# Query transposes moved to other places of a row pair, weights turned earlier, two tap groups read together, and a tail's second rows asked earlier, in an E-Branchformer kernel

## The chip, the cores and the metric

One NeuronCore of a Trainium2 chip. The time is the device time of one launch in microseconds (us); medians and ranges are over several launches. The profile is one launch taken by the hardware profiler. Times in it count from the start of its span.

The engines: PE is TensorE's matmuls and PEld its weight loads, DVE is VectorE, ACT is ScalarE, POOL is GpSimd, and SP is the engine whose queue asks for most transfers. "L2057" is a line of the kernel. The changed kernel's lines stand one or two further down. Names such as X, pD, Sm or dhr are the program's own tiles: in the attention stage the PE writes scores to pS and pD, ACT and DVE make Pm and Sm of them, the PE adds products of these up in X ("X fills"), and acc takes X up. In a tail, gs and ug are rows that are read, dhr is the gradient dh read back, and EF and gr are sums for the weights' gradients.

## The reference

Forward and backward pass of one E-Branchformer layer (two batches, 4000 tokens, 144 channels, bf16), with the gradients of the input and of all seven weights:

```python
def _fwd_reference(x, w_qkv, w_att_out, w_mlp_in, dw_csgu, w_mlp_out, dw_merge, w_merge):
    xa = _layernorm(x)
    q, k, v = split(xa @ w_qkv)                       # cut
    attn = softmax(q @ k.T * D ** -0.5) @ v
    glob = attn @ w_att_out
    u, g = split(gelu(_layernorm(x) @ w_mlp_in))
    g = _layernorm(g); gc = sum of 5 shifted g * dw_csgu      # cut
    loc = (u * gc) @ w_mlp_out
    m = concat(glob, loc); m = m + (5 shifted m * dw_merge)   # cut
    return x + m @ w_merge
# reference(): the output and jax.vjp's gradients for x and the weights
```

## The kernel before

Each batch goes through three stages: a head, the attention stage (two thirds of the time), and a tail. The parts that the change touches, cut:

**Places.** In the attention stage, row blocks of 128 are worked in pairs of 16 places. At each place the PE does its fixed work, and a small scheduler may add one step of a task: of the local branch or of the query transposes.

```python
class Steps:
    def place(self, tensor=True):
        ...
            due = [t for t in self.tasks if t[1] is not None and (t[1][0] == 'P' or t[1][0] == 'L' and self.now % 2) and self._ready(t)]
            if due:
                self._step(min(due, key=lambda t: t[0]))
        self.now += 1
...
        def jit(g):                       # query transposes, 7 a batch
            ...
            for step in range(3):
                yield 'P', 2
                ...
                pj = ps_f.tile([128, 4, 128], BF, tag="f", name="pj")
                for j in range(4):
                    nc.tensor.transpose(pj[:, j, :], src[:, j, :], id_[:])
                nc.scalar.copy(jt[g][step][:], pj[:])
...
        # (row block of 0..7 half places) -> X fills (number, rows); three PSUM banks in all
        fills = {(0, 1): ((0, (0,)), (1, (0,))), (1, 0): ((0, (1,)), (1, (1,))), (1, 1): ((2, (0, 1)),), (2, 1): ((3, (0, 1)),), ...}
```

Three PSUM banks serve the X fills, the transposes and the local steps, least recently used first. Fills 0 and 1 of a pair are opened at place 1 and closed at place 2. Even fills are added up by DVE (`acc<-X,acc`), odd ones by ACT and POOL.

**The tail** runs in program order:

```python
            loads(0)                 # gs and ug rows of group 0
            load_dh(0)               # dhr: dh back from DRAM
            load_dh(1)
            loads(1)
            ...
            for h in range(NPR + 5):
                g, hf = divmod(h, 2)
                if 0 < h < NPR:
                    turn_dx2(*turn_dx(h))        # transposes of dhr and others
                if hf == 0 and 0 <= g - 2 < NGR - 1:
                    fill(g - 2)                  # reads r<-y and r<-u on ACT's queue
                if h == NPR + 1:
                    fill(NGR - 1)
                ...
                if h == NPR - 1:
                    spill_ef()                   # ACT copies EF out of four banks; gr takes two of them
```

**The head** of the first batch turns the weights and builds products of them:

```python
        # heads()
        WlT = self.turn(self.Wl, D, 0, D, "w_lT", pst)
        # phase_head: order of the first steps
                wts.heads(ps_t, ps_2, lambda: nrm.stats(0))
                nrm.power(0)
                wts.taps1(0)          # POOL: w_A<-w_lT,w_wr
                wts.keys(ps_t, ps_2)  # turns w_q and w_k, then the fused M
                nrm.shift(0)
                narrow(0)             # POOL: g<-gs, the narrow rows
                nrm.apply(0)
                wts.taps()            # DVE: w_A<-w_voT,w_wr, w_Bz
```

## Time and profile before

| | before |
|---|---|
| time, median of 3 (range) | 1273.08 us (1272.24 to 1273.53) |
| profiled span | 1269.4 us |
| PE busy | 1206.0 us, 95% |
| granted PE clock | 0.997; 1.00 in every stage, lower only after 1262 us |
| attention stages | 68 to 545 and 683 to 1155 us |
| PE waits for X behind DVE's acc | 4.4 us a stage |

How to read it: 95% of PE time is in use, so only its gaps are to be had. Lines such as `PE X L2057 <- DVE acc L2073` name the waiting instruction and what it waited for. The lines themselves are shown in the prediction below.

### The profile page before, as it was taken

To read this page: it belongs to the slowest core of one execution; us is meant where nothing else is said; L and a number is where in the kernel's file an instruction comes from. 1 tells how busy PE (TensorE), PEld (TensorE's weight loads), DVE (VectorE), ACT (ScalarE), POOL (GpSimd) and SP (SyncE) were. 2 spreads that over 40 slices of the span, in tenths; PEclk is the share of its full clock that TensorE was granted. 3 is DMA by queue.
4 is the path that set the end of the run, shared out by engine and by line. 5 is a ranking of instruction groups with operands and counts; after the bars stand their busy time and mean duration, and the time that the engine had idled before them with its cause. 6 is when DMAs were issued, how large, how long until landed. Compare 5 with 4: busy or idle time off the path is not lost.

```text
span 1269.4 us, 39810 instructions
## 1 busy us (share of the span) xinstructions
PE 1206.0 (95%) x15118; PEld 946.8 (75%) x15118; DVE 962.5 (76%) x3261; ACT 843.4 (66%) x2494; POOL 558.3 (44%) x1007
## 2 busy tenths in 40 slices
PE   7999999999999999989999999999999999998996
PEld 4667777777777777789886777777777777778984
DVE  7567788888788887857646678888888878875774
ACT  5777767776777666546567777777776776654542
POOL 7323444544445533357512254544544445325650
PEclk9999999999999999999999999999999999999998
DMA  7479898889998999978857998999898999998861
GB/s 212 100 142 179 147 157 159 161 150 159 162 160 149 164 164 157 158 205 218 222 160 139 156 162 143 155 161 170 152 166 155 157 163 154 158 162 197 243 172 25
DMA packets 633616, 205.43 MB, mean 162 GB/s; under 512 B 576719, under 2 KB 630948, under 8 KB 633380
## 3 DMA queue, kind: packets, MB, share of 16 engines
q1 hardware_dynamic: 626912, 197.46, 82.6%
q10 hardware_dynamic: 6500, 5.32, 1.8%
q8 instruction: 120, 1.97, 0.6%
q14 instruction: 84, 0.69, 0.2%
HBM read 46.11 MB, written 21.79 MB: 53 GB/s over the span
## 4 chain that ended last, share of the span: by engine, by line
PE 71%; DVE 13%; DMA 4%; ACT 4%; issue 4%; POOL 1%; SPq 0%; ACTq 0%; DVEq 0%; POOLq 0%
PE y L2035 15%; PE pS L1989 9%; PE X L2057 8%; PE X L2058 8%; PE pD L1989 7%; DVE Sm L1999 5%; PE pS L1985 5%; PE pb L1518 3%; PE pc L1693 2%; PE EF L2193 2%; PE po L2218 2%; DVE jg L1916 2%; DMA ug<-ug_d 1%; PE gr L2289 1%; DVE acc L2073 1%
## 5 line engine op out<-in xcount | busy, mean ns | idle before, releaser
L1999 DVE SCALAR_TENSOR_TENSOR Sm<-pD,Pm 128x500 bf16<-128x500 f32 x512 | 325.7, 673 | 81.3 <-PE pD L1989 46.0
L1997 ACT ACTIVATE Pm<-pS 128x500 bf16<-128x500 f32 x512 | 295.8, 586 | 39.4 <-PE pS L1989 36.3
L2057 PE MATMUL X<-Qs,Sm 128*128 128x144 bf16 x2048 | 285.8, 226 | 9.3 <-DVE acc L2073 8.9
L2070 POOL TENSOR_TENSOR acc<-xs,acc 128x432 f32<-128x432 f32 x150 | 168.5, 1124 | 281.7 <-ACT xs L2069 281.3
L2058 PE MATMUL X<-Bt,Pm 128*128 128x144 bf16 x2048 | 285.6, 226 | 0.8 <-DVE Bt L2022 0.8
L2058 PEld LDWEIGHTS <-Pm 128*128 128x128 bf16 x2048 | 200.2, 98 | 11.9 <-issue 11.4
L2057 PEld LDWEIGHTS <-Sm 128*128 128x128 bf16 x2048 | 200.1, 98 | 1.6 <-issue 1.0
L2035 PEld LDWEIGHTS <-PT 128*128 128x128 bf16 x2048 | 136.6, 98 | 31.0 <-issue 3.0
L2035 PEld LDWEIGHTS <-ST 128*128 128x128 bf16 x2048 | 136.4, 98 | 27.6
L2069 ACT COPY xs<-X 128x432 f32<-128x432 f32 x150 | 78.0, 520 | 111.6 <-PE X L2058 103.3
L2073 DVE TENSOR_TENSOR acc<-X,acc 128x432 f32<-128x432 f32 x180 | 104.0, 578 | 54.3 <-PE X L2058 53.7
L1997 ACT ACTIVATION_READ_ACCUMULATOR Pm<-pS 128x1 f32 x512 | 104.7, 205 | 0.0
L1985 PE MATMUL pD<-rb,QBr 16*128 16x500 bf16 x448 | 95.5, 378 | 4.0 <-DVE Sm L1999 3.5
L1989 PEld LDWEIGHTS <-BTm 128*128 128x128 bf16 x512 | 49.8, 98 | 59.9 <-issue 1.6
L1985 PE MATMUL pS<-rb,QBr 16*128 16x500 bf16 x448 | 91.9, 379 | 0.3
L1916 DVE SCALAR_TENSOR_TENSOR jg<-gnC,dgC 128x256 bf16<-128x256 bf16 x160 | 90.8, 568 | 1.2
L2045 POOL TENSOR_TENSOR B_t<-zd,yd 128x144 bf16<-128x144 f32 x64 | 34.1, 533 | 112.5 <-ACT zd L2044 112.2
L1989 PEld LDWEIGHTS <-QTm 128*128 128x128 bf16 x512 | 29.0, 97 | 72.2 <-issue 72.2
L1989 PE MATMUL pS<-ra,QTm 128*128 128x500 bf16 x256 | 76.5, 380 | 0.0
L1989 PE MATMUL pS<-rb,QTm 128*128 128x500 bf16 x256 | 76.5, 380 | 0.0
L2035 PE MATMUL y<-ra,PT 128*128 128x144 bf16 x1024 | 74.3, 226 | 1.4 <-ACT zd L2044 1.4
L2035 PE MATMUL y<-rb,PT 128*128 128x144 bf16 x1024 | 74.3, 226 | 1.4 <-ACT zd L2044 1.4
(638 smaller groups left out, 2878.6 us busy)
## 6 DMA issues: line engine op xcount, KB each, us to landing
gs<-in_grad_out_dram SPq DMA_DIRECT2D x24, 720.0 KB
dh_d<-dh SPq DMA_DIRECT2D x32, 144.0 KB
dhr<-dh_d SPq DMA_DIRECT2D x16, 288.0 KB
gs<-in_grad_out_dram SPq DMA_DIRECT2D x8, 540.0 KB
xg<-in_x_dram SPq DMA_DIRECT2D x21, 144.0 KB
dug_d<-dug SPq DMA_DIRECT2D x16, 144.0 KB
dug<-dug_d SPq DMA_DIRECT2D x32, 72.0 KB
ug_d<-ug SPq DMA_DIRECT2D x32, 72.0 KB
```

Source lines behind the costliest of these rows:

```text
L1518: nc.tensor.matmul(pb[:], goT[:, i * 128 + m:i * 128 + m + 128], W.GL[:, m, :, :].rearrange("p a b -> p (a b)"), start=(m == 0), stop=False)
L1916: nc.vector.scalar_tensor_tensor(jg[:], a_[:, m:m + 256], 1.0, d_[:, 2:258], op0=ALU.mult, op1=ALU.mult, accum_out=dws[:, p, m:m + 1])
L1985: nc.tensor.matmul(o_[h][:, 0:SC], jt[i // 4][2][rr, i % 4, :], S.XR[c2][rr, 0:SC], start=True, stop=False)
L1989: nc.tensor.matmul(o_[h][:, 0:SC], jt[i // 4][w][:, i % 4, :], S.xaT[:, c0:c0 + SC], start=False, stop=True)
L1997: nc.scalar.activation(P[:, pb, c1:c1 + SC], o_[h][:, 0:SC], ACT.Exp, accum_out=ld8[:, 0, n_:n_ + 1])
L1999: nc.vector.scalar_tensor_tensor(Sm[:, pb, c1:c1 + SC], o_[h][:, 0:SC], 1.0, P[:, pb, c1:c1 + SC], op0=ALU.mult, op1=ALU.mult, accum_out=l ...
L2035: nc.tensor.matmul(y[:, w, :], src[:, jj, :], S.xaa[:, j, :], start=(j == 0), stop=(j == NBK - 1))
L2057: nc.tensor.matmul(X[:, jj, :], Sm[:, i % NP, j * 128:(j + 1) * 128], Qs[:, i % 4, :], start=(kk == 0 and jj == 0), stop=False, skip_group ...
L2058: nc.tensor.matmul(X[:, jj, :], P[:, i % NP, j * 128:(j + 1) * 128], Bt[:, i % 4, :], start=False, stop=(kk == 1), skip_group_check=True)
L2069: nc.scalar.copy(xs[:, 0:nj, :], X[:, 0:nj, :])
L2070: nc.gpsimd.tensor_tensor(a_, xs[:, 0:nj, :], a_, op=ALU.add)
L2073: nc.vector.tensor_tensor(a_, X[:, 0:nj, :], a_, op=ALU.add)
```

## The change

Four parts, with their intents: (A) turn the query and key weights while another weight is still on its way; (B) keep the query transposes from the places where X fills hold two of three banks; (C) read the last two tap groups together, before the EF copies; (D) ask for the tail's second group of rows first.

```diff
@@ heads(), keys()                                               (A)
+        self.WqT = self.turn(W.Wqkv, D, 0, D, "w_qT", pst)
+        self.WkT = self.turn(W.Wqkv, D, D, D, "w_kT", pst)
         WlT = self.turn(self.Wl, D, 0, D, "w_lT", pst)
...
-        WqT = self.WqT = self.turn(W.Wqkv, D, 0, D, "w_qT", pst)
-        WkT = self.WkT = self.turn(W.Wqkv, D, D, D, "w_kT", pst)
+        WqT, WkT = self.WqT, self.WkT
@@ place(), jit()                                                (B)
-   ... t[1][0] == 'L' and self.now % 2) and self._ready(t)]
+   ... t[1][0] == 'L' and self.now % 16 > 2) and self._ready(t)]
...
-                yield 'P', 2
+                yield 'L', 1
@@ phase_tail()                                                 (D)
             loads(0)
+            loads(1)
             load_dh(0)
             load_dh(1)
-            loads(1)
...                                                              (C)
-                if hf == 0 and 0 <= g - 2 < NGR - 1:
+                if hf == 0 and 0 <= g - 2 < NGR - 2:
                     fill(g - 2)
-                if h == NPR + 1:
-                    fill(NGR - 1)
...
                 if h == NPR - 1:
+                    fill(NGR - 2)
+                    fill(NGR - 1)
                     spill_ef()
```

More of the change, by code (lines that the diff above doesn't have):

```diff
@@ L1766, in place @@
         if tensor:
-            due = [t for t in self.tasks if t[1] is not None and (t[1][0] == 'P' or t[1][0] == 'L' and self.now % 2) and self._ready(t)]
+            due = [t for t in self.tasks if t[1] is not None and (t[1][0] == 'P' or t[1][0] == 'L' and self.now % 16 > 2) and self._ready(t)]
             if due:
```

## The prediction

The "up to 0.4 us" for four issues is the author's estimate; in the profile before, the ACT queue's four reads between 619 and 624 us took 0.32 to 0.67 us each to ask.

> **What bounds the kernel now.** I read the page's busy shares first, then the chain of waits, then windows of the PE per stage, then the waits of the PE inside a long stage, and last the single instructions around the commonest of these waits. Busy shares and chain:
>
> ```profile
> PE 1206.0 (95%) x15118; PEld 946.8 (75%) x15118; DVE 962.5 (76%) x3261; ACT 843.4 (66%) x2494; POOL 558.3 (44%) x1007
> PE 71%; DVE 13%; DMA 4%; ACT 4%; issue 4%; POOL 1%; SPq 0%; ACTq 0%; DVEq 0%; POOLq 0%
> ```
>
> TensorE (PE) is busy 1206.0 of a span of 1269.4 us, and 71% of the chain is its own work. The change removes no matmul, so at most the 63.4 us of PE idle time are to be had. The windows say where they lie (columns: window, length, PE busy and count, weight loads, DVE, ACT, POOL, then clock and DMA):
>
> ```profile
> 545.00:560.00 15.00, 12.09 (x192) 11.44 (x190) 5.30 (x19) 7.18 (x15) 8.00 (x23) 1.00 0.75 229
> 620.00:645.00 25.00, 22.80 (x336) 21.64 (x336) 10.62 (x39) 11.96 (x32) 8.86 (x20) 1.00 0.82 249
> 100.00:200.00 100.00, 98.31 (x1207) 74.36 (x1206) 76.79 (x247) 73.21 (x218) 42.26 (x73) 1.00 0.92 157
> 1235.00:1270.00 35.00, 21.90 (x269) 16.44 (x266) 16.36 (x70) 8.49 (x26) 0.00 (x0) 0.89 0.13 31
> ```
>
> The attention stages (68 to 545 and 683 to 1155 us), where most of the time passes, have 2 to 4% of PE gaps. The densest gaps are in the starts of the tails, in the first 16 us (6.8 us idle) and in the last 35 us (13.1 us idle); the change doesn't touch the last. Waits of the PE in the first attention stage (columns: waiting line, releaser, us in total, times, longest):
>
> ```profile
> PE X L2057 <- DVE acc L2073: 4.4, 6, 1.7
> PE pD L1985 <- DVE Sm L1999: 2.9, 12, 0.5
> PE ph L1809 <- ACT dgC L1669: 1.4, 1, 1.4
> PE y L2035 <- ACT zd L2044: 1.4, 1, 1.4
> PE pc L1693 <- ACT gc L1867: 0.9, 1, 0.9
> ```
>
> The second stage has the same list within 0.1 us. One such X wait, on the PE and on DVE in the same stretch:
>
> ```profile
> 198.64 0.39 PE L1965 MATMUL pj<-w_ident,Q_t 128*128 128x128 bf16 x4
> 199.79 0.22 PE L2057 MATMUL X<-Qs,Sm 128*128 128x144 bf16 x1 [0.76 <-DVE acc L2073]
> ```
> ```profile
> 197.94 0.67 DVE L1999 SCALAR_TENSOR_TENSOR Sm<-pD,Pm 128x500 bf16<-128x500 f32 x1
> 198.54 0.67 DVE L1999 SCALAR_TENSOR_TENSOR Sm<-pD,Pm 128x500 bf16<-128x500 f32 x1
> 199.13 0.60 DVE L2073 TENSOR_TENSOR acc<-X,acc 128x432 f32<-128x432 f32 x1
> ```
>
> X fills, transposes and local steps share three PSUM banks. Fills 0 and 1 of a row pair hold two of them until place 2 of the pair's 16. The transposes (pj) then took the third, and fill 2 needs the bank of fill 0, whose evacuation stands on DVE behind two Sm of 0.67 us. The PE stood 0.76 us.
>
> [...] 288 KB of dhr alone took 2.7 us from issue to landing, and 4.2 us when gs followed it at once.
>
> **The change, part by part.**
>
> **Query transposes** (seven a batch, three groups of four each). They took place 2 of a pair in six of seven; by the instruction order of the changed kernel they now start at place 3 or later, none at 0 to 2. Removed: from the start-to-start times of the PE, stalls between such a transpose and fill 2 come to 9.5 us in 12 cases over both batches, 4.7 us a batch (the waits view has 4.4). Given back: fill 2 still lands on fill 0's bank in 6 pairs of a batch, by the changed order, instead of 9, because other local steps go to place 2 more often (7 instead of 4). The cases before in which a small step stood ahead cost 0.57 and 0.66 us. For the three cases more of this kind that the order shows, some 0.5 us each: 1.5 us. Four transposes a batch now take the bank of X0 directly and one that of X1; they come a place later, so I take 0.2 us each: 1 us. Small tiles that follow a small tile into the same bank one place later fall from 8 to 1; the ph wait of 1.4 us and the pc wait of 0.9 us may be of that kind. I count half of them, 1.1 us. Net per batch: 4.7 − 1.5 − 1.0 + 1.1 = 3.3 us, 6.6 us over two. I take 5, since in a stage with the PE at 98% a wait removed tends to come back elsewhere: the 2.9 us of pD behind Sm show DVE close behind.
>
> **Last two tap groups.** Fill 6 was read by ACT's queue one step later. Before, this read of r was asked at 622.52 (ACT's transfer before it was still in flight until 622.44), landed at 626.36, and the PE waited:
>
> ```profile
> PE po L2219 <- DMA r<-u: 1.8, 1, 1.8
> PE EF L2193 <- POOL g L2155: 1.7, 2, 0.9
> PE EF L2193 <- DMA ug<-ug_d: 1.6, 2, 1.2
> ```
>
> (waits of the PE, 543 to 645 us.) Asked at about 620 to 621, it lands around 624 to 625, ahead of need. Four issues now precede the EF copies on ACT, which can cost up to 0.4 us. The second tail had no such wait. Sum: 1.8 − 0.4, so 1.4 us.
>
> **A tail's second group of rows.** The SP queue at the start of the first tail:
>
> ```profile
> 547.05 0.32 SPq L2151 DMA_DIRECT2D dhr<-dh_d  x1
> 550.12 0.32 SPq L1905 DMA_DIRECT2D dh_d<-dh  x1
> 550.49 0.42 SPq L2151 DMA_DIRECT2D dhr<-dh_d  x1
> 551.00 0.41 SPq L1112 DMA_DIRECT2D gs<-in_grad_out_dram  x1
> 551.47 0.49 SPq L2147 DMA_DIRECT2D ug<-ug_d  x1
> ```
>
> The gs and ug rows (720 and 144 KB) stood behind a dhr that waited for the last dh store. They landed at 556.54 and 558.17, and the PE waited 1.2 us for ug. In the changed order they go ahead of both dhr; asked about 3 us earlier, ug lands well before need: 1.2 us gone here, 0.8 in the second tail with its gs and ug waits. But the first dhr then stands behind 864 KB. gs and ug took 1.9 and 1.6 us between landings, so dhr lands some 3.5 us later than 549.74, near 553; its transposes ran at 551.34. New wait: 0 to 2 us, 1 in the mean, in each tail. Net: 2.0 − 2.0, so 0 ± 3 for both.
>
> **Turns of the weights.** At the start the PE waits 2.5 us for w_l, until 7.60. The turns of w_q and w_k now run in that wait instead of after it, and DVE's copies at 8.79 and 9.45 move forward, which clears some 1.2 us of DVE. The POOL chain after it (w_A 8.45, ra 11.09, rstdx 14.62) starts from w_l and keeps its place. I take 0.4 us of the 1.2.
>
> Sum: 5 + 1.4 + 0 + 0.4 = 6.8 us. From 1273.1 that is 1266.3; I name 1267, since part of the PE's short waits are absorbed before the next longer wait.
>
> **The rivals.** First, the wait moves: local steps at place 2, or transposes at place 3 in X0's bank, pay for the same eviction. For it: 6 of 16 pairs still have fill 2 on fill 0's bank, and DVE is 77 to 81% busy in the stages, so its queue is seldom empty. Against it: the odd fills are evacuated by ACT (0.52 us), which is less loaded at 66%. Then the time is 1271 to 1273. Second, the early rows starve dhr: the PE waits in each tail for its first transposes of dh, 2 to 4 us, and POOL's product of dhr behind them. For it: 549.74 leaves only 1.6 us of room before 551.34. Against it: the early request may go out while dh is still being stored, and in 545 to 560 the PE is only 81% busy, so a shift is partly swallowed. With the first part working, 1269 to 1271; with neither, 1275. Third, all of it holds: both stages lose their X and small-tile waits (4.4 + 1.4 + 0.9 each), the y wait of 1.4 us moves away, and tails lose their row waits: 1258 to 1262. Against it: the y wait is a chain through ACT and DVE which no part touches.
>
> **Range and chances.** Runs of the kernel before spread over 1.3 us. The sum's terms span from about zero (first and second rival) to 15 us. I predict 1267 us, with 1260.5 to 1273.5 to hold 8 times in 10. Faster by over 2% needs 25.5 us out of 63.4 us of idle time; not even the third rival gives it: 0.01. Slower by over 2% needs a new wait of 0.8 us (25.5 over 32) in every pair of the two batches, for which nothing speaks: 0.01. Within 2%: 0.98.
>
> **What would show it.** The waits of the PE in the attention stages should show X behind DVE's acc below 2 us a stage instead of 4.4, and no pj just before a fill 2. If a ph, pc or pj wait behind acc of like size stands there, the first rival holds. In the first tail, the r wait of 1.8 us should be gone, and so should the ug wait; a wait for dhr ahead of the dh transposes of over 2 us is the second rival. At the start, the PE's work after 10 us should shift by less than 1.2 us. I'm wrong if the stages' lengths change by under 1 us each, or by more than 6 us, or if a tail grows by over 2 us. PE busy time should stay at 1206 us.

## More of the kernel before

**The local branch** writes its gradient `dh` in two halves, in three buffers, and stores it. The step that writes the first half for pair p may run as soon as the second half of pair p-3 is written:

```python
        yield 'V', 2, aft(("dh", 3)), 1.1
        dh = wk.tile([128, 2, 2 * D], BF, tag="dh", bufs=3, name="dh")
        ...
        nc.vector.tensor_tensor(dh[:, :, 0:D], du[:], gp[:, :, 0:D], op=ALU.mult)
        ...                                    # steps later
        nc.vector.tensor_tensor(dh[:, :, D:2 * D], dg[:], gp[:, :, D:2 * D], op=ALU.mult)
        nc.sync.dma_start(S.dh_d[:, 2 * p:2 * p + 2, :], dh[:])
        Q.mark("dh", p)
```

## The result, and the profile after

The changed kernel took 1288.08 us (median of 4, 1286.80 to 1290.87) against 1273.11 us: the ratio is 1.0121, with a 95% interval of 1.0104 to 1.0139. Ratios here are the mean time of one kernel's runs over the mean of the other's of the same rounds, so not quite the ratio of the medians. It is slower by 15 us, and the prediction's range ended at 1273.5.

The busy shares and the chain of waits of the changed kernel:

```profile
PE 1222.9 (95%) x15118; PEld 955.5 (74%) x15118; DVE 971.7 (75%) x3261; ACT 842.1 (65%) x2494; POOL 559.6 (43%) x1007
PE 67%; DVE 16%; DMA 6%; ACT 4%; issue 4%; POOL 1%; SPq 1%; ACTq 0%; DVEq 0%; POOLq 0%
```

The PE has as many matmuls as before (15118) but is busy for 16.9 us more. Its idle time (span less busy) went only from 63.4 to 66.1 us. The same matmuls took longer, so one looks at the granted clock. It was 0.986 instead of 0.997. Two windows at the start of the first tail (columns as in the prediction: window, length, busy times, clock, DMA):

```profile
557.46:560.88 3.42, 0.28 (x3) 0.17 (x3) 0.31 (x1) 0.00 (x0) 0.24 (x2) 1.00 1.04 323
560.88:564.29 3.41, 3.36 (x31) 3.30 (x30) 0.15 (x1) 1.01 (x1) 1.25 (x5) 0.50 1.08 378
```

A window of 3.42 us with almost no matmul (PE busy for 0.28 us) is followed by one of 3.41 us at half clock (0.50). The records of the clock show eight such half-clock windows between 16 and 1240 us, of 3.413 us each: at 21.6, 79.6, 519.9, 560.9, 636.0, 700.8, 1141.1 and 1182.1 us. The profile of the kernel before has none. (This profile is the slowest of the four launches; over the launches the clock lost, one less the granted share, comes to 13.5 us on average, of which some 3.4 us are the end of the program, as in the profile before, 6.7 us at half clock.)

The waits of the PE in the windows 0 to 68, 68 to 545, 545 to 600 and 600 to 690 us of the changed kernel:

```profile
PE tp L1483 <- POOL g L1438: 3.2, 1, 3.2
...
PE pD L1986 <- DVE Sm L2000: 5.8, 16, 2.1
PE X L2058 <- DVE acc L2074: 3.5, 4, 1.2
...
PE pt L2205 <- DMA dhr<-dh_d: 3.2, 1, 3.2
...
PE gr L2290 <- ACT EFs L2278: 3.1, 1, 3.1
```

X behind acc fell from 4.4 to 3.5 us, and in the first tail the waits for r and for ug that the prediction counted are gone. In their place stand four single waits of 2.1 to 3.2 us that the kernel before did not have. Each has a cause that another engine's records show.

**g (part A)**, GpSimd at the start:

```profile
8.35 3.70 POOL L1254 TENSOR_TENSOR w_A<-w_lT,w_wr 128x720 bf16<-128x720 bf16 x1 [1.20 <-DVE w_lT L1139]
12.13 0.46 POOL L1438 TENSOR_SCALAR g<-gs 128x320 bf16<-128x320 bf16 x1
```

Before, this w_A took 1.39 us, beside small copies on DVE. With the turns moved, DVE starts its own w_A and w_Bz at 8.47 us and runs them to 10.8, and GpSimd's w_A takes 3.70 us. The 2.3 us added are as long as those products of DVE. Why GpSimd's instruction lasts longer beside them is not shown. Its record starts first (8.35 against 8.47 us); GpSimd's records are rough, though.

**pD (part B)**, DVE and then the PE:

```profile
517.86 1.05 DVE L1878 TENSOR_TENSOR dh<-du,gp_t 128x288 bf16<-128x288 bf16 x1 [4.23 <-DMA dh_d<-dh]
518.84 0.67 DVE L2000 SCALAR_TENSOR_TENSOR Sm<-pD,Pm 128x500 bf16<-128x500 f32 x1
```
```profile
519.57 0.37 PE L1986 MATMUL pD<-rb,QBr 16*128 16x500 bf16 x1 [2.06 <-DVE Sm L2000]
```

The write of dh waited 4.23 us for the store of the dh whose buffer it takes. The Sm behind it in DVE's queue came late, and the PE stood 2.06 us for the bank that Sm reads. In the second batch it is the same, with 2.17 us.

**dhr (part D)**, the SP queue at the start of the first tail:

```profile
549.03 5.52 SPq L1906 DMA_DIRECT2D dh_d<-dh  x2
554.83 0.38 SPq L1112 DMA_DIRECT2D gs<-in_grad_out_dram  x1
555.27 0.50 SPq L2148 DMA_DIRECT2D ug<-ug_d  x1
555.82 0.90 SPq L2152 DMA_DIRECT2D dhr<-dh_d  x2
```

The rows stand behind the last store of dh (asked at 554.20). Counted from the stage's last X fill they still went out 3.0 us earlier than before: gs was asked 1.3 us after it, not 4.2. The first dhr, which before went out ahead of that store, now stands behind the store and 864 KB. It landed at 560.56, 7.0 us after the last X fill instead of 2.95, and the PE had waited since 557.4.

**gr (part C)**, ACT and its queue at the end of the first tail:

```profile
631.01 0.31 ACTq L1648 DMA_DIRECT2D r<-y  x1
633.42 0.31 ACTq L1648 DMA_DIRECT2D r<-u  x1
633.77 1.36 ACT L2278 COPY EFs<-EF 128x432 f32<-128x432 f32 x3 [4.12 <-DMA r<-y]
```

The third and fourth read were asked only at 631.01 and 633.42, 0.02 and 0.03 us after transfers of the next batch's rows landed (xg at 630.99, gs at 633.39) that carried the same completion semaphore. ACT's queue stood meanwhile, and the EF copies behind it began 7.2 us after the last EF instead of 2.95; gr takes banks that they free, and came 3.2 us late. It is the same in C alone, where the third and fourth read were asked 0.02 us after such transfers landed. The kernel before has it too: its read of r at 622.52 stood until gs (asked on the SP queue at 618.42, same semaphore) landed at 622.44.

Where the time came from, as differences of the same program points in the two profiles: up to the first X fill +3.8 us (two half-clock windows in it); first attention stage +3.0 (one); to the first dhr transposes of the first tail +2.5; to the end of its EF +0.1 (one); to gr +3.2; to the first X fill of the second batch +1.6 (two); second attention stage +3.1 (one); to the dhr transposes +2.9; the rest −0.4 (one). Together 19.6 us, of which eight half-clock windows at half of 3.41 us could be up to 13.7 (an estimate). Not all eight belong to the change. Five follow a window that holds a new wait for pD, dhr or gr. Those at 21.6, 79.6 and 700.8 us do not, and kernels that leave these stretches as they were have such windows at the same places (below; for the last one, 684.5 and 684.8 us in two of the mended kernels).

### The profile page after: what moved, and what is told of

Its sections match the earlier page's. It is cut to its first block, busy times and chain, and to the rows that moved or that the text cites. A ratio compares the mean times of both kernels' runs of the same rounds, so it can differ in the third digit from the quotient of the medians.

```text
span 1289.0 us, 39788 instructions
## 1 busy us (share of the span) xinstructions
PE 1222.9 (95%) x15118; PEld 955.5 (74%) x15118; DVE 971.7 (75%) x3261; ACT 842.1 (65%) x2494; POOL 559.6 (43%) x1007
## 4 chain that ended last, share of the span: by engine, by line
PE 67%; DVE 16%; DMA 6%; ACT 4%; issue 4%; POOL 1%; SPq 1%; ACTq 0%; DVEq 0%; POOLq 0%
PE y L2036 15%; PE pS L1990 9%; PE X L2058 8%; PE X L2059 8%; PE pD L1990 7%; DVE Sm L2000 6%; PE pS L1986 5%; PE pb L1519 3%; PE pc L1694 3%; PE po L2219 1%; DVE jg L1917 1%; DVE acc L2074 1%; PE gr L2290 1%; PE pD L1986 1%; DMA dhr<-dh_d 1%
## 5 line engine op out<-in xcount | busy, mean ns | idle before, releaser
L1986 PE MATMUL pD<-rb,QBr 16*128 16x500 bf16 x448 | 99.7, 379 | 8.5 <-DVE Sm L2000 8.0
L1917 DVE SCALAR_TENSOR_TENSOR jg<-gnC,dgC 128x256 bf16<-128x256 bf16 x160 | 93.7, 586 | 0.9
L2025 POOL TENSOR_SCALAR nr<-nd,rl 128x1 f32<-128x1 f32 x64 | 16.9, 263 | 139.0 <-DVE nd L2018 138.2
L2019 ACT ACTIVATE Qs<-Q_t,rl 128x144 bf16<-128x144 bf16 x64 | 26.5, 415 | 76.0 <-DVE rl L2016 75.8
```

The source lines that it names most:

```text
L1917: nc.vector.scalar_tensor_tensor(jg[:], a_[:, m:m + 256], 1.0, d_[:, 2:258], op0=ALU.mult, op1=ALU.mult, accum_out=dws[:, p, m:m + 1])
L1986: nc.tensor.matmul(o_[h][:, 0:SC], jt[i // 4][2][rr, i % 4, :], S.XR[c2][rr, 0:SC], start=True, stop=False)
```

## The experiments

Two theories. **The clock theory**: a new long wait is followed by a window at half clock, as at 560.88 us above (3.41 us at 0.50), so it costs its length and up to 1.7 us more (an estimate: half of 3.41 us). **The wait theory**: only the new waits count, and the half clock falls into idle time. Every kernel below gave correct results. Each was timed in five rounds against the kernel before.

### The four parts, one by one

Edits: hunk (A), (B), (C) or (D) of the diff above, alone on the kernel before.

A: 

> Only the early turns of the query and key weights. Two theories are tested by the four single parts. [...] Wait theory: only the new waits count, the half clock falls into idle time. In the changed kernel this part's stretch, up to the first X fill, grew by 3.8 us, with two half-clock windows in it. Both theories: GpSimd's first w_A takes near 3.7 us in place of 1.39 (beside VectorE's w_A) and the PE waits some 3 us for g. Clock theory: +3 to +5 us in all, with one to three half-clock windows. Wait theory: +0.5 us.

B: 

> Only the query transposes moved. In the changed kernel each attention stage grew by 3.0 us from first to last X fill, with one half-clock window in it after a PE wait of 2.1 us: VectorE's write of dh stood 4.2 us for an earlier dh store on the SP queue, with Sm behind it. Clock theory: about +6 us in all[...]. Wait theory: +2.6 us. If the wait for dh comes from another part, the stages get shorter, by 2 to 3 us each.

C: 

> Only the last two tap groups read together. In the changed kernel the PE stood 3.05 us in the first tail before gr, because ScalarE's queue stood 4.1 us at the fourth read and the copies of EF came after it; the wait for r of 1.8 us went. Clock theory: +3 us (3.1 less 1.8 plus 1.7 for one half-clock window). Wait theory: +1.3 us. The second tail: no change.

D: 

> Only the order of loads at a tail's start. In the changed kernel the first dhr was asked after the last dh store and behind 864 KB, and the PE stood 3.2 and 3.6 us before the transposes of dh. Clock theory: +5 us (some 2.5 us of wait in each tail, 1.7 for each half-clock window, less 1.6 in each for the ug and gs waits that went). Wait theory: +2 us. Half-clock windows at these two places only.

| part | median us (range) | ratio (95%) | the wait named, in its profile | half-clock windows before 1240 us |
|---|---|---|---|---|
| A | 1274.58 (1274.15 to 1278.98) | 1.0020 (1.0000 to 1.0040) | g 3.3 us; GpSimd's w_A 3.69 us | 2 |
| B | 1277.92 (1275.66 to 1281.01) | 1.0041 (1.0019 to 1.0062) | pD up to 2.1 and 2.5 us | 2 single, 1 double |
| C | 1276.62 (1271.80 to 1279.88) | 1.0029 (1.0005 to 1.0053) | gr 3.4 us | 2 |
| D | 1279.09 (1277.12 to 1284.50) | 1.0053 (1.0030 to 1.0075) | dhr 3.3 and 2.6 us | 2 single, 1 double |

Every wait came back with its own part alone, so each part causes its own wait. The four excesses add up to 1.43%, against 1.21% for the whole. All four times lie nearer to what the clock theory expected, or above it; A is between the two, at 2.5 us. But the intervals are wide: those of A, B and C (0.0 to 5.1, 2.4 to 7.9 and 0.6 to 6.7 us) hold the wait theory's figure too, and only D's (3.8 to 9.5) does not.

For A the profile goes further. Its first projection (pq) comes only 0.6 us later than in the kernel before (21.88 against 21.28 us), since the 3.3 us for g largely stand in place of other waits. The other 3.1 us up to the first X fill are two half-clock windows (from 21.5 and 79.5 us), and the next section shows such windows in kernels that leave the head as it was. That A's wait brought them is not shown.

### What a half-clock window costs, and when it came

These profiles hold a comparison. From its first projection (pq) to the first X fill, ten of the kernels (all that were compared) run the same 497 PE instructions in the same order; among them are the kernel before, C alone and group 6 alone (below). C alone, then group 6 alone, two windows each:

```profile
73.86:77.27 3.41, 2.92 (x13) 0.90 (x12) 2.14 (x10) 2.06 (x8) 1.69 (x2) 1.00 0.97 202
77.27:80.68 3.41, 3.41 (x19) 2.19 (x19) 2.28 (x8) 2.50 (x8) 0.00 (x0) 0.50 1.20 195
```
```profile
74.65:78.06 3.41, 3.15 (x14) 1.06 (x14) 2.15 (x7) 2.06 (x7) 1.02 (x1) 1.00 0.91 192
78.06:81.47 3.41, 3.41 (x43) 2.53 (x41) 2.26 (x9) 3.11 (x11) 1.00 (x5) 1.00 1.43 164
```

In C the next window ran at half clock: 19 matmuls in it instead of 43. The stretch took 59.91 us there, and 58.31 and 58.30 us in the kernel before and in group 6 alone. The other seven agree: 58.28 us without a half-clock window (the hold alone), 59.91 to 59.96 with one (B, D, D filled, the store on another queue), and 61.13 and 61.38 with two (B with the hold, and A). So one half-clock window cost 1.6 us in this stretch, where the PE is the bound (busy for 2.92 to 3.41 us of each window above), without any longer wait. Most of these kernels don't touch this stretch, so their changes don't explain why a window came in one profile and not in another.

What brings it on is not shown by the busy time: the window before it has the PE busy for 2.92 of 3.41 us in C, with 13 matmuls, and half clock followed; in group 6 alone it is 3.15 us, with 14, and the clock stayed at 1.00. The length of a wait alone doesn't decide either: in the changed kernel a pD wait of 2.06 us ended at 519.57 us, and half clock followed from 519.92; in B alone the same wait of 2.06 us ended at 517.72, and none followed. What does decide is not shown by these views. The kernel before has no half-clock window before 1262 us in its profile, but its launches vary too: beside the four parts their median was 1272.43 us, one at a clock of 0.993 took 1277.17 us, and one at 0.997 took 1270.94.

The launches agree with a cost of that kind: within each kernel's own launches (158 in all), a launch's time goes with the clock it lost, by 0.75 us for each us lost (standard error 0.06; the clock is recorded to three digits, about 1.3 us, which makes this low rather than high). That shows that the two go together, not which of them is the cause.

### Filling the wait for dhr

Part D, with 40 transposes of no use into the same bank ahead of the first dhr transposes:

```diff
             pt = ps_t.tile([128, 8, 128], BF, tag="tp", name="pt")
+            for n_ in range(40 if p == 0 else 0):
+                nc.tensor.transpose(pt[:, n_ % 8, :], S.Yn[:, n_ % 4, 0:128], id_[:])
             for q in range(2):
```

> The tail's loads in the changed order, with 40 matmuls of no use (transposes of rows that lie ready, some 2.3 us at full clock, overwritten in the same bank) ahead of the first transposes of dhr, inside the wait for dhr of 3.3 and 2.6 us. No data comes sooner and the PE has more to do. Clock theory: the half-clock windows at the two tail starts (6.8 and 3.4 us long with the loads alone) go, and the time falls 3 to 5 us below that of the loads alone, to +1.5 to +3.5 us against the kernel before. Wait theory: the time stays that of the loads alone, +6.7, or grows.

(The 2.3 us are an estimate: in the kernel before, eight such transposes start from 551.34 to 551.73 us, 0.056 us apart, so 40 take some 2.2 us.)

Measured: 1281.39 us (1279.19 to 1283.91), ratio 1.0057 (1.0038 to 1.0076). In its profile the half-clock windows at both tail starts are gone, as the clock theory had it (in the first the clock is 1.00 from 552 to 562.2 us, where D alone has 0.50 from 555.16 to 561.99; the records have others, at 77.6, 630.5 and 1064.0 us). But the time did not fall below that of D alone (1.0053). From the first dhr transposes to the last EF the first tail got 1.3 us shorter and the second 0.6 us, while in the second these transposes themselves came 0.9 us later. Its launches lost 6.8 us of clock on average, those of D alone 9.4. So the expectation failed. In these tails the half clock was not, or not fully, on the path that sets the end. The 1.6 us of the stretch above, where the PE is the bound, can't be counted for each window in a tail.

### Only the order of dhr and rows

```diff
             load_dh(0)
+            loads(1)
             load_dh(1)
-            loads(1)
```

> The second group's rows are asked between the first and the second dhr instead of ahead of both. If it was the order of dhr and rows that cost, the wait for dhr goes from 3.3 and 2.6 us to under 0.5, the waits for ug and gs stay smaller than in the kernel before, and the time is -0.5 to -2 us against it. If the early request itself costs[...], dhr is still waited for by 1 us or more, and the time is above that of the kernel before by 2 us or more.

Measured: 1275.41 us (1273.08 to 1281.81), ratio 1.0011 (0.9992 to 1.0031). Waits for dhr of 2.2 and 1.8 us stand in its profile (taken of its slowest launch, 1281.81 us). They are not for the first dhr, which landed 2.69 us after it was asked, as in the kernel before, and was not waited for. They are for the second, which is now asked behind the 864 KB:

```profile
555.06 0.42 SPq L2151 DMA_DIRECT2D dhr<-dh_d  x1
```
```profile
561.67 0.40 PE L2204 MATMUL pt<-w_ident,dhr 128*128 128x128 bf16 x2 [2.17 <-DMA dhr<-dh_d]
```

It landed at 561.62, 6.6 us after it was asked. So the order was most of D's cost (1.0053 to 1.0011), and the wait moved from the first dhr to the second. The gain expected did not come.

### Group 6 alone read earlier

```diff
-                if hf == 0 and 0 <= g - 2 < NGR - 1:
+                if hf == 0 and 0 <= g - 2 < NGR - 2:
                     fill(g - 2)
...
                 if h == NPR - 1:
+                    fill(NGR - 2)
                     spill_ef()
```

> Only group 6 is read a step earlier, ahead of the copies of EF; group 7 stays in its old place. If it was the third and fourth read, standing in ScalarE's queue ahead of the EF copies, that made gr wait, then gr doesn't wait here (3.4 us with both read together), the wait for r is under 0.5 us, and the time is -1.5 to -2 us against the kernel before. If two reads ahead of the copies are already too many, gr still waits 1 us or more.

Measured: 1275.07 us (1270.71 to 1276.15), ratio 0.9999 (0.9978 to 1.0020). The gr wait and the r wait are both gone, and the first tail's last gr came 2.1 us earlier. The next head then waited 2.1 us for DVE's go80f, which in turn stood 2.6 us for a transfer, and a half-clock window followed at 641.3 us. So the third and fourth read were part C's cost, and what part C was to gain is taken back in the next head: the wait moved. The gain expected did not come.

### The narrow rows first on GpSimd

Part A, and:

```diff
-                wts.taps1(0)
                 wts.keys(ps_t, ps_2)
                 nrm.shift(0)
                 narrow(0)
                 nrm.apply(0)
+                wts.taps1(0)
```

> The early turns, with GpSimd making g (the narrow rows) and its share of ra ahead of its first w_A. If it was GpSimd's w_A beside VectorE's w_A (3.7 us in place of 1.39) that made g late, the wait of 3.3 us of the PE for g goes, the first X fill comes at or up to 1 us before that of the kernel before, unless a window before it stays at half clock, and the time is 0 to -1.5 us. If the wait only moves (to w_A of the rows, read by the PE later), a wait of 1 us or more for w_A or w_GL stands there and the time is +1 or more.

Measured: 1274.26 us (1273.55 to 1276.04), ratio 1.0006 (0.9989 to 1.0023). The wait for g fell from 3.3 to 1.6 us, and the waits for ra came to 3.4 us (2.7 us in the kernel before); half clock of double length (6.8 us) stood in its profile, at 19.1 us. GpSimd's g, now the first beside DVE's products, took 2.06 us instead of 0.46. So the longer time beside DVE's products moved from w_A to g itself, the wait fell by half, and nothing was gained over the kernel before.

### The store of dh on another queue, and its control

```diff
-        nc.sync.dma_start(S.dh_d[:, 2 * p:2 * p + 2, :], dh[:])
+        nc.gpsimd.dma_start(S.dh_d[:, 2 * p:2 * p + 2, :], dh[:])
```

With part B: 

> The moved query transposes, with the store of dh asked by GpSimd's queue instead of the SP queue, so that it no longer stands behind the transposing transfers there. If it was the store standing in the SP queue that held VectorE's next dh, and with it Sm and the PE for 2.1 to 2.5 us a batch, the longest wait of pD for Sm falls to 0.6 us or less, and the time falls by 3 us or more against the moved transposes alone (1277.9, +5.5), to about +1 to +2.5. If the wait for dh has another cause, a wait of pD of about 2 us stays and the time stays near +5.

Alone: 

> Control: the kernel before with only the store of dh moved to GpSimd's queue. The kernel before has no wait of DVE on that store of over 1 us, so both theories have it at 0 +- 1.5 us; a larger cost would be that of asking on GpSimd's queue, and is to be taken off the run with the moved transposes.

Measured: with B 1284.88 us (1279.33 to 1288.30), ratio 1.0087 (1.0066 to 1.0109); alone 1277.61 us, ratio 1.0037 (1.0021 to 1.0053). The control failed too: asking on GpSimd's queue cost 0.4% here by itself, with 6.7 us of X waits in the first stage instead of 4.4. Taken off, B remains at 0.5%. DVE's dh still waited 4.0 us for the store. My first reading, a store that stands in the SP queue, was at most half of it: in the changed kernel the store was asked 2.3 us after the write of dh (512.89 to 513.20, asked at 515.53), on GpSimd's queue 0.3 us after it, and DVE waited about as long. The records show the order instead: DVE writes the second half of one dh at 514.43 and comes to the first half of the dh in the same buffer right after it, with the store of 4 us in between, on whichever queue. In the kernel before, these two lie 4.3 us apart with other work between.

### All local steps off places 1 and 2

```diff
-   ... (t[1][0] == 'P' or t[1][0] == 'L' and self.now % 2) and self._ready(t)]
+   ... t[1][0] in 'PL' and self.now % 16 not in (1, 2) and self._ready(t)]
...
-                yield 'P', 2
+                yield 'L', 1
```

> All local steps and the query transposes kept off places 1 and 2 of a pair, where X fills 0 and 1 hold two banks. Rival of the prediction (the local steps at place 2 now pay for the same bank): the waits of X for acc, 3.5 and 3.0 us a stage with the query transposes alone moved, fall under 1 us, and unless dh's store stands in the way again the stages get 1 to 3 us shorter than before, the time -2 to -5. If the bank isn't what these waits are about (VectorE is simply late), X still waits 3 us or more a stage, from other fills.

With the store on GpSimd's queue: 

> The same with the store of dh on GpSimd's queue. If both readings hold, this is the fastest: X waits under 1 us a stage and no pD wait over 0.6 us, the time -3 to -6 us. If the waits move to other steps (ph, pc, pj behind acc, by the same sum), the time is within 1.5 us of the kernel before.

Measured: 1295.78 us, ratio 1.0185 (1.0168 to 1.0202), and 1298.76 us, ratio 1.0207 (1.0185 to 1.0229). The second's X wait (2.9 us) and pD wait (up to 1.6 us) were above what was expected too. The waits of the PE, 68 to 600 us, of the first:

```profile
PE pt L2169 <- ACT dgf L1891: 6.6, 1, 6.6
PE X L2057 <- DVE acc L2073: 5.3, 1, 5.3
```

The single X wait left is that one; the others inside the stage are gone, and pc and ph wait 2.3 us for acc in all. So much fits the prediction's first rival, that small steps pay for the same banks. But the local steps, with two places fewer, no longer finish within the stage: its last ones run alone, with the PE waiting 6.6 and 5.3 us; from the last X fill to the first dhr transposes it takes 13 us longer in both batches. So this form failed for another reason than the one it was to test.

### Holding the write of dh

Part B, and:

```diff
-        yield 'V', 2, aft(("dh", 3)), 1.1
+        yield 'V', 2, tuple(((n_, p - 3), 3) for n_ in ("dh",) if p >= 3), 1.1
```

> The moved query transposes, with the step that writes the first half of dh held until three places (about 1.7 us each) after the second half of the dh three pairs before, whose buffer it takes. With the store on another queue the wait stayed, because the two halves follow each other on VectorE with the store's 4 us between them. If that order is the cause, the wait of VectorE for dh's store and the longest wait of pD (2.1 to 2.5 us) go, with the half-clock windows behind them, and the time falls 3 to 5 us below the moved transposes alone, to +0.5 to +2.5 us. If the pD wait stays, or another local step makes one of like size, the cause is still another.

The same hold alone on the kernel before, as a control: 

> Control: the kernel before with only the hold of three places on the step that writes dh. If the -5.7 us of moved transposes and hold together come from the transposes (fewer bank waits of X, no small-tile waits of ph and y), this is 0 +- 1.5 us. If the hold itself is what gains, -4 us or more.

Measured: B with the hold 1266.52 us (1263.79 to 1267.87), ratio 0.9948 (0.9932 to 0.9964); the hold alone 1272.68 us (1270.53 to 1275.35), ratio 0.9997 (0.9981 to 1.0012). DVE with B and the hold, and the waits of its PE, 68 to 545 us:

```profile
512.13 0.31 DVE L1904 TENSOR_TENSOR dh<-dgf,gp_t 128x288 bf16<-128x288 bf16 x1
...
517.26 0.91 DVE L1877 TENSOR_TENSOR dh<-du,gp_t 128x288 bf16<-128x288 bf16 x1 [0.28 <-DMA dh_d<-dh]
```
```profile
PE pD L1985 <- DVE Sm L1999: 3.4, 14, 0.4
PE X L2057 <- DVE acc L2073: 3.0, 3, 1.2
```

The wait for the store is 0.28 us, and no pD wait is over 0.4. The time fell not by the 3 to 5 us expected but by 11 against B alone, and is 0.5% below the kernel before. In the profiles the two attention stages, from first to last X fill, are 3.5 and 7.0 us shorter than in B alone, and 1.9 and 2.2 us shorter than in the kernel before. The half-clock window of double length behind B's second pD wait (1131 us) is gone; those at 20.9 and 78.9 us, which this part doesn't touch, stand in this profile. The control shows that the hold alone gains nothing. So the moved transposes gain, once dh isn't in the way.

### Mended parts together, and the whole change with the hold

Edits: B with the hold and group 6 alone; the same with A and the narrow rows first; and the whole change with the hold.

> The same with group 6 alone read a step earlier. The parts of the change added up so far (15.3 us of the whole against 18.5 of the four alone), so this should be the run above plus 0 to +0.5 us (group 6 alone measured 0.9999). Faster than the kernel before by 1 us or more only if removing the bank waits was worth something once dh no longer stands in the way.

> The same with the early weight turns in the form with the narrow rows first on GpSimd (1.0006 alone): three parts of the change, each mended, and the fourth left out. If the causes named are right and complete, within 2.5 us of the kernel before, instead of +15; if something of the change's cost is still unnamed, +4 us or more.

> The whole change with only the hold added. The moved transposes went from +5.5 to -5.7 with it. If the parts add up, the whole goes from +15 to +3 to +6 us; the waits of the PE for dhr (some 3 us in each tail), gr (3 us) and g (3 us) stay. If the half clock is brought on mostly by the attention stages' waits, it is at the lower end; +8 or more would mean that the other three parts cost more together than alone.

Measured: 1266.89 us, ratio 0.9957 (0.9942 to 0.9972); 1266.77 us, ratio 0.9956 (0.9941 to 0.9970); and 1278.90 us, ratio 1.0041 (1.0026 to 1.0057). The two mended ones are faster than was expected, since B with the hold is, and add nothing to it. The whole change with one scheduling condition more goes from +15 to +5 us, within its expectation. The best version is B with the hold alone; of the other parts none gained.

## Why the prediction was wrong, point by point

**Bound and idle time.** Right that the PE bounds the kernel and that its gaps are all there is to gain. Wrong that its busy time would stay at 1206 us. The prediction read a clock of 1.00 in the windows and took it as given. The step that fails is in every term: a wait was counted at its length only. In the changed kernel five half-clock windows followed new waits, of 2.06 us at the least, and one such window cost 1.6 us where the PE is the bound (59.91 against 58.30 us for the same instructions). One reading beside it was off: DVE is 77 to 85% busy in the windows of 100 us from 100 to 500, not 77 to 81.

**Query transposes, −5 us.** Alone +5.2 us (1.0041 of 1273). With the hold it came to −0.5%, 6.6 us, of which the control takes nothing. So the direction was right; that the size agrees is in part luck. The waits listed for a stage fell by 3.0 us (12.7 to 9.7), near the 3.3 worked out, but by other terms: X's waits fell only to 3.0 us, not under 2, while the ph and y waits of 1.4 us and the pc wait for gc of 0.9 us went whole (ph and pc were half counted, y not at all), and new pc waits of 0.9 us behind acc and 0.5 us more of pD came. The stages themselves are only 1.9 and 2.2 us shorter in the profile. The rest of the 6.6 us would lie in the tails, where untouched stretches of other profiles differ as much (the hold alone: −1.6 us from the first dhr transposes to the last EF in the first tail, +2.8 in the second). What failed is that the term looked only at the bank. Moving a task changes which local steps share a place, and here it brought two halves of dh together that share a buffer. The changed order of DVE's instructions, which could be read beforehand, had it.

**Last two tap groups, −1.4 us.** Measured +3.7 us (1.0029). The r wait went, as worked out. The step "Four issues now precede the EF copies on ACT, which can cost up to 0.4 us" failed: it counted the asking, while ACT's queue stood for earlier transfers to land; gr then waited 3.4 us. The sign was in the prediction's own trace: what was in flight until 622.44 was not ACT's transfer before it (that landed at 623.42) but gs on the SP queue, which carried the same semaphore. The kernel with group 6 alone shows both that this was the cause, and that the 1.8 us are given back in the next head.

**The second group's rows, 0 ± 3 us.** Measured +6.7 us (1.0053). The second rival is what happened, and its waits of 2 to 4 us in each tail were right in size: 3.3 and 2.6 us in D alone. That the rows are "asked about 3 us earlier" held for gs: counted from the stage's last X fill it was asked at 1.3 us instead of 4.2, in the whole change and in D alone (ug at 1.7 and 3.7 instead of 4.7), and the first tail has no wait for ug left. The step that failed is the new wait for dhr, "0 to 2 us, 1 in the mean". The working had dhr behind the 864 KB alone; it also fell behind the last dh store, which it had been ahead of. It landed 4.0 us later than before, counted from the same point, in the whole change and 5.0 in D alone, where 3.5 was worked out. And 3.5 less the 1.6 us of room is 1.9 us by the prediction's own figures, not 1.

**Turns of the weights, −0.4 us.** Measured +2.5 us (1.0020; the interval begins at zero). That the POOL chain "keeps its place" failed: GpSimd's w_A went from 1.39 to 3.69 us beside the products of the DVE that had been freed, and g began at 12.0 us instead of 9.9. In its profile the first pq was 0.6 us later; the rest, up to the first X fill, is two half-clock windows, of which it isn't shown that A brought them.

**The rivals and the chances.** The prediction named a wait that moves and a starved dhr, and gave both at most +2 us. That all four parts could lose at once was in neither. That nothing speaks for a loss of over 2% came out true (the loss was 1.2%), but the range left no room above the old time.

**What stays open.** How much of the whole change's 15 us is clock and how much is wait. Its launches lost 13.5 us of clock on average, those of the kernel before in the later rounds 6.2. At 0.75 to 1 us of time for each us lost, the difference is 5 to 7 us, an estimate; the filled tail shows that in a tail it can be less. The rest would be the waits. Why the first half of the tail, without the half clock, still took as long in D filled was not followed further. What A costs apart from half-clock windows that also come without it is open too.

## What to carry to other kernels

When a task moves in a tuned schedule, read the changed order of every engine for buffers that are written again soon after a store, not only for the resource that the move is about. Ahead of a transfer queue, ask what the queue itself will stand for: a request put earlier in the text may only push another one back. And on a kernel bound by the PE, look at the granted clock in windows of a few us: here a single new wait of 2.06 us was followed by 3.41 us at half clock, and such a window cost 1.6 us where the PE was the bound. The version worth keeping is the moved transposes with the hold on dh, at 0.9948.
